# A transformer kernel on one core: the exponentials' buffers split into two rings, and the planner that orders the work given new margins

## The chip, the core and the metric

The kernel runs on one NeuronCore of a Trainium2 chip. TensorE (PE) multiplies matrices into PSUM (eight banks of 128 x 512 fp32), VectorE (DVE) and ScalarE (ACT) read PSUM and write on-chip memory (SBUF), GpSimd (POOL) works on SBUF alone, and SyncE (SP) issues most DMA transfers. The metric is the device time of one execution in microseconds (us); lower is better. The time given for a kernel is the median of several runs.

## The reference, cut to what matters

Two layers, each attention and then a gated feed-forward, with the same weights twice. x is 2048 x 512, there are 32 heads of 16, and F is 1792.

```python
for _ in range(2):
    h = layernorm(x)
    q, k, v = split_heads(h @ wqkv)                    # 32 heads of 16
    p = softmax(q @ k.T * 16 ** -0.5)                  # 2048 x 2048 per head
    x = x + merge_heads(p @ v) @ wo
    h = layernorm(x)
    x = x + (gelu_tanh(h @ w_gate) * (h @ w_up)) @ w_down
```

The exponentials are the bulk of it: 32 heads x 2048 x 2048 in each layer, 268 million in all.

## The kernel before, in words

**Tiles and units.** A *tile* is the scores of 128 keys against 512 queries of one head, one PSUM bank. A *unit* is a block of 512 queries and a group of four heads: 16 key tiles x 4 heads = 64 tiles. A layer has 4 x 8 = 32 units, the kernel 64 units and 4096 tiles. The last eight units are run as two halves of 256 queries each (parts F0 and F1), where a tile holds two key tiles of 256 queries. The four heads of a group lie in four strips of 32 rows of the PE array (j = 0 to 3), so up to four score matmuls (L1548) run side by side.

**Score slots and the two ways to an exponential.** Banks 0-2 and 3-4 are two *slots*, filled in turn with three and two tiles. ACT takes a whole slot in one instruction (L1562), 128 x 1536 or 128 x 1024, and writes bf16 exponentials to `fPT`. A fill can carry one tile more, in a bank of its own (5 or 6), which is VectorE's: L1602 turns the scores into int16 that, read as float16, are a piecewise linear exponential (`fPI`), and L1642 makes three shifted copies of up to four such tiles at once (`fPP`). Which tiles may go this way is fixed (`d_able`: every third, 20 of 64), and whether one does is decided by `vector_tile`. A tile of ACT needs one PV matmul (L1694, exponentials times V, with a 17th column of ones for the softmax's sums), a tile of VectorE needs four (one from `fPI`, three from `fPP`). PV matmuls of the four heads run side by side in four column strips and accumulate in bank 7.

**Partial sums.** When a unit's last PV matmul is done, DVE copies bank 7 to a buffer of `fOS` (L1000; L995 adds a part that was stored before). From there DMAs store it (`oscr`), gather its sums (`fLT`), and DVE inverts these; `fRB` is the inverse spread back over the rows, and POOL multiplies (L956). The buffer is free again when its four stores have landed. In layer 2 the first twelve units are begun before the last block of layer 1 is done: their part A goes to DRAM (`ascr`) and comes back into an `fOS` buffer for part B.

**Feed-forward pieces.** After the attention of a block of 512 queries, a *post* works off its output projection, layer norm, gate (L1222, evacuated by L1241), gelu (L1509 on ACT, after all 14 gate tiles), up (L1222, evacuated by L1265), and down (L1286, with one bank held over seven pieces of two matmuls: an *open down tile*). A post is cut into *pieces* of mostly four 512-column matmuls, which PE runs between the fills of the next block's attention. After the last exponential comes the feed-forward of the last half block (F1), with gelu in ScalarE's evacuation (L1244).

**The planner.** The order of the instructions on each engine is not written out. `_emit_fast` runs a loop (from L1844) that keeps a modelled clock for each engine, picks what PE does next, and emits it; DVE, POOL and SP get their jobs in modelled order of readiness. What is emitted is a fixed program: each engine runs its list in order and waits on semaphores for true dependencies. So the constants of the model change the order of the program and nothing else. The ones that the change touches:
- `dma` and `turn` (L282 to L297): the modelled landing of a transfer, which decides when work that needs it is put into the order.
- `vector_tile` (L1400): a DVE tile is taken while DVE's modelled backlog, with 0.39 us for every waiting shift, is under `DVE_LATE`. `pick` (L1422) also asks that `behind() < LAG`.
- `behind` (L1808): by how much (in us of PE work) the running post is behind its even pace (`PACE`, `LAST`).
- the loop's choices (L1865 to L1912): a fill goes as soon as its slot and its `fPT` buffer are free; else PE may work until `limit`, which is the later of the next fill's readiness and ScalarE's modelled end less 0.6 us. PV rounds come first if they fit (`fit`) and if four full rounds are there; then a piece, if it fits within `limit` plus a tolerance (`p.tol`, `post_tol`); then the PV that is left; then, if the array's density over the last 3.4 us is under `DENSE`, `keep_clock` (L1708): four matmuls of zeros (L1714, *fillers*), which keep TensorE's clock up.
- `fPT` has seven buffers of 1536, and each slot takes the next one, whether it has two tiles or three; `fOS` has seven.

Of the kernel before, what the change touches and what calls it, by code (L numbers as in the profile page):

```python
# [6 lines left out]
BF = mybir.dt.bfloat16  # L7
# [168 lines left out]
def _emit_fast(nc, es, x_in, wqkv, wo, wg, wu, wd, out, n_rep=2):  # L176
# [24 lines left out]
    DVE_LATE = 2.0  # L201
# [29 lines left out]
    NPT = 7  # L231
    PT = sb("fPT", [128, NPT, 1536], BF)
# [6 lines left out]
    NOS = 7  # L239
# [39 lines left out]

    wire = [0.0]  # L280

    def dma(eng, grp, dst, src, r=(), w=(), serial=False, kb=32):  # L282
        if grp not in sch.groups:
            sch.add_dma_group(grp, serial=serial)
        t = max(sch.free[eng], sch.ready(eng, r, w)) + 0.5
        wire[0] = max(t, wire[0]) + kb / 280.0
        return sch.op(eng, lambda e: e.dma_start(dst, src), r=r, w=w, grp=grp, cost=0.5, lat=wire[0] - t + 1.3)
# [3 lines left out]
    def turn(grp, dst, src, r, w):  # L291
        if grp not in sch.groups:
            sch.add_dma_group(grp, serial=True)
        t = max(sch.free["sp"], sch.ready("sp", r, w)) + 1.2
        wire[0] = max(t, wire[0]) + 128 / 180.0
        return sch.op("sp", lambda e: e.dma_start_transpose(dst, src), r=r, w=w, grp=grp, cost=1.2,
                      lat=wire[0] - t + 0.6)  # L297
# [286 lines left out]
    def xn(i, alt):  # L584
        if alt == "late":
            return PT[:, i, 0:D].bitcast(F16)
        return HT[:, i + 4 * alt, 0:D].bitcast(F16)
# [791 lines left out]
    LAG = 16.8  # L1379
    PRE = 1  # L1380
    pt_no = [0]
    dg = {"n": 0, "items": [], "uk": None, "done": [0]}
# [80 lines left out]
    def fill_ready():  # L1463
# [11 lines left out]
        if pend.get(("PT", pt_no[0] % NPT)):  # L1475
            return None
# [53 lines left out]
    def a_slot(atiles, dtile):  # L1530
# [6 lines left out]
        p = pt_no[0] % NPT  # L1537
# [24 lines left out]
        o = sch.op("act", lambda e: e.activation(PT[:, p, 0:512 * na].rearrange("p (a b) -> p a b", a=na),  # L1562
# [15 lines left out]
        for k, x in enumerate(atiles):  # L1578
            add(x, o.seen, PT[:, p, 512 * k:512 * (k + 1)], [("PT", p)], ("PT", p))
# [196 lines left out]
    def post_source():  # L1776
        while True:
            if posts:
# [62 lines left out]
    DENSE = 0.7  # L1841
    log = {"idle": 0.0, "warm": 0}

    while True:  # L1844
# [25 lines left out]
        stuck[0] = F is None and not (pend.get(("PT", pt_no[0] % NPT)) and left())  # L1870
# [12 lines left out]
        press = F is None and left() and pend.get(("PT", pt_no[0] % NPT)) or shifts and pend.get(("PP", shifts[0][0]))  # L1883
# [891 lines left out]
```

## Time and profile before

| | us |
|---|---|
| median of 9 runs (1609.57 to 1613.55) | 1612.09 |
| the profiled execution, its own time | 1615.17 |
| its span, first to last instruction | 1613.3 |
| VectorE busy | 1420.0 (88%) |
| GpSimd busy | 179.1 (11%) |
| first exponential starts / last one ends | 17.88 / 1578.34 |
| matmuls of zeros (L1714) | 1420 |
| score matmuls that ACT's fills and DVE's tiles come from (L1548) | 4608 |
| PV matmuls from `fPT`, `fPP`, `fPI` | 3589, 3057, 1019 |
| mean granted TensorE clock | 0.995 |

The page gives, for each engine, busy time and share of the span; then slices of the span, the DMA queues, the chain of work that ended last, and groups of instructions by line, with the mean length of one in ns and the idle time of the engine just ahead of them. "Busy" of a group is time covered, so instructions that overlap on an engine count once, while a mean is each one's own length. A waiting time put down to "PE fPS L1548" means that the scores came late. "Issue" is time without a wait that the trace shows. 16 DMA engines move 70 GB/s on average, and their packets fill about a quarter of their time.

### The profile page before, as it was taken

The numbers are of one execution on the slowest core, as the hardware profiler recorded it, in microseconds if no ns is written. First come the engines' busy times: TensorE is split into PE (matmuls) and PEld (weight loads), VectorE is DVE, ScalarE is ACT, GpSimd is POOL, SyncE is SP. The second block draws the span as 40 slices with busy tenths as digits, with TensorE's granted clock in tenths as the row PEclk, the third lists the DMA queues.
The fourth block names the chain that finished last, engine by engine and source line by source line (L and its number), as shares of the span: only waits on it lengthen the run. The fifth ranks groups of instructions, "written<-read, shape, count | busy, mean of one in ns | idle before, by whom it ended". The sixth has DMA issues, their size and how long they took to land.

```text
span 1613.3 us, 38435 instructions
## 1 busy us (share of the span) xinstructions
PE 1521.3 (94%) x16176; PEld 505.9 (31%) x16176; DVE 1420.0 (88%) x2428; ACT 1535.4 (95%) x1321; POOL 179.1 (11%) x218
## 2 busy tenths in 40 slices
PE   8999999998999999999999999889999999999998
PEld 3332222222222222332332223222222222444445
DVE  7899999879989899888999889998888988998784
ACT  6999999999999999999999999999999999999992
POOL 3311010011100021001411001010001000200000
PEclk8999999999999999999999999999999999999999
DMA  5200111233111251123311233332313113213235
GB/s 154 60 5 8 49 35 48 56 87 78 47 47 38 65 122 34 38 60 104 87 47 60 66 97 75 88 102 76 99 35 96 48 50 114 61 44 88 64 98 156
DMA packets 168376, 112.39 MB, mean 70 GB/s; under 512 B 55048, under 2 KB 148232, under 8 KB 168200
## 3 DMA queue, kind: packets, MB, share of 16 engines
q1 hardware_dynamic: 164504, 105.28, 24.5%
q0 software_dynamic: 2112, 4.19, 1.0%
q8 instruction: 131, 2.15, 0.6%
q10 hardware_dynamic: 1584, 0.39, 0.1%
q14 instruction: 45, 0.37, 0.1%
HBM read 81.40 MB, written 19.78 MB: 63 GB/s over the span
## 4 chain that ended last, share of the span: by engine, by line
ACT 43%; PE 42%; DVE 10%; DMA 2%; issue 1%; POOL 1%; SPq 0%; DVEq 0%; POOLq 0%
ACT fPT L1562 39%; PE fPS L1694 13%; PE fPS L1548 12%; PE fPS L1222 8%; PE fPS L1286 5%; DVE fPI L1602 4%; DVE fPP L1642 4%; PE fPS L653 3%; ACT fHT L1509 3%; DMA fRB<-rscr 1%; PE fPS L1714 1%; DMA fXNT<-fHT 1%; ACT L1509 1%; ACT L1562 0%; PE fPS L730 0%
## 5 line engine op out<-in xcount | busy, mean ns | idle before, releaser
L1562 ACT ACTIVATE fPT<-fPS 128x1536 bf16<-128x1536 f32 x1276 | 1459.0, 1281 | 39.9 <-PE fPS L1548 34.9
L1602 DVE TENSOR_SCALAR fPI<-fPS 128x512 int16<-128x512 f32 x908 | 616.6, 685 | 88.8 <-PE fPS L1548 82.5
L1548 PE MATMUL fPS<-fQ,fKT 32*128 32x512 f16 (+1 forms) x4608 | 510.9, 360 | 52.7 <-ACT fPT L1562 34.2
L1642 DVE TENSOR_SCALAR fPP<-fPI 128x2048 int16<-128x2048 int16 (+3 forms) x753 | 471.7, 654 | 9.4 <-PE fPS L1694 4.4
L1694 PE MATMUL fPS<-fPT,fVP 128*17 128x512 bf16 (+1 forms) x3589 | 465.0, 359 | 10.8 <-DVE fOS L995 3.7
L1694 PE MATMUL fPS<-fPP,fVD 128*17 128x512 f16 (+1 forms) x3057 | 424.6, 358 | 3.9 <-DVE fPP L1642 2.6
L1548 PEld LDWEIGHTS fPS<-fQ,fKT 32*128 32x128 f16 x4608 | 137.2, 91 | 531.4 <-ACT fPT L1562 376.4
L1694 PE MATMUL fPS<-fPI,fVP 128*17 128x512 f16 (+1 forms) x1019 | 266.1, 359 | 1.6 <-DVE fOS L1000 0.9
L1222 PE MATMUL fPS<-fXNT,fWR 128*128 128x512 f16 (+1 forms) x952 | 220.3, 363 | 8.2 <-DVE fHT L1265 3.5
L1694 PEld LDWEIGHTS fPS<-fPT,fVP 128*17 128x17 f16 x3589 | 120.1, 88 | 146.7 <-issue 92.3
L1694 PEld LDWEIGHTS fPS<-fPP,fVD 128*17 128x17 f16 x3057 | 116.2, 89 | 117.4 <-issue 59.3
L956 POOL TENSOR_TENSOR fAT<-fOP,fRB 128x512 f16<-128x512 f32 (+1 forms) x35 | 41.9, 1197 | 850.8 <-DMA fRB<-rscr 839.8
L1286 PE MATMUL fPS<-fWR,fHT 128*128 128x512 bf16 x428 | 118.7, 383 | 0.3 <-DVE fPI L1602 0.2
L1714 PE MATMUL fPS<-fONB,fZV 128*17 128x512 f16 x1420 | 117.2, 386 | 1.5 <-POOL fQMASK L380 1.5
L1222 PEld LDWEIGHTS fPS<-fXNT,fWR 128*128 128x128 bf16 x952 | 77.0, 98 | 112.4 <-DVE fPI L1602 26.3
L1265 DVE TENSOR_TENSOR fHT<-fPS,fHT 128x512 bf16<-128x512 f32 x112 | 76.4, 689 | 37.0 <-PE fPS L1222 26.9
L1241 DVE CAST fHT<-fPS 128x512 bf16<-128x512 f32 x105 | 71.5, 686 | 16.8 <-PE fPS L1222 16.8
L1694 PEld LDWEIGHTS fPS<-fPI,fVP 128*17 128x17 f16 x1019 | 67.4, 89 | 38.0 <-issue 18.5
L743 POOL TENSOR_SCALAR fVD<-fVP 128x544 f16<-128x544 f16 (+1 forms) x48 | 57.1, 1190 | 167.6 <-DVE fVP L751 165.0
L605 POOL TENSOR_SCALAR fLNS<-fMV 128x2 f32<-128x2 f32 (+1 forms) x28 | 11.6, 416 | 363.8 <-DVE fMV L596 363.3
L1000 DVE COPY fOS<-fPS 128x512 f32<-128x512 f32 (+1 forms) x72 | 45.1, 626 | 7.6 <-PE fPS L1694 6.5
L701 DVE TENSOR_SCALAR fQ<-fPS,fQMASK 128x512 f16<-128x512 f32 (+1 forms) x72 | 46.3, 684 | 1.3 <-PE fPS L653 1.2
(89 smaller groups left out, 638.8 us busy)
## 6 DMA issues: line engine op xcount, KB each, us to landing
fWR<-in_B_w_up_dram SPq DMA_DIRECT2D x62, 256.0 KB, 2.9
fWR<-in_B_w_down_dram SPq DMA_DIRECT2D x58, 256.0 KB, 2.8
fWR<-in_B_w_gate_dram SPq DMA_DIRECT2D x57, 256.0 KB, 4.9
oscr<-fOS SPq DMA_DIRECT2D x224, 32.0 KB, 1.7
fOP<-oscr SPq DMA_DIRECT2D x28, 256.0 KB, 2.8
fRB<-rscr SPq DMA_DIRECT2D x28, 256.0 KB
fX<-in_A_x_dram POOLq DMA_DIRECT2D x4, 1024.0 KB, 6.4
xscr<-fX SPq DMA_DIRECT2D x16, 256.0 KB, 2.1
```

The lines of the kernel that those rows point to most:

```text
L743: job("pool", 2, [(lambda e, dst=dst, src=src, ph=ph: e.tensor_scalar(dst, src, 2.0 ** (-ph / NPH), None, op0=ALU.mult), [("VP", c, k) for ...
L1222: ins = e.matmul(bank(bs[0])[:, w * qn:(w + 1) * qn], lhsT=wchunk(s, (ft + w) % 2, ck), rhs=XNT[:, ck, xs], start=(ck == 0), stop=(ck == N ...
L1241: evac_job(1, b, [(lambda e: e.tensor_copy(in_ht(ft), in_bank(b)), [BK[b]], fk, 0.6)], got(("gate", layer, qb, h, ft)))
L1265: (lambda e: e.tensor_tensor(in_ht(ft), in_bank(b), in_ht(ft), op=ALU.mult), [BK[b]] + fk, fk, 0.62)], got(("up", layer, qb, h, ft))))
L1286: ins = e.matmul(bank(b)[:, 0:D], lhsT=HT[:, ft, i * 128:(i + 1) * 128], rhs=wslot(s)[:, jj * D:(jj + 1) * D], start=(ft == 0), stop=(ft = ...
L1509: sch.op("act", lambda e, lo=lo, hi=hi: e.activation(HT[:, lo:hi, q0:q0 + qn], HT[:, lo:hi, q0:q0 + qn], ACTF.Gelu_apprx_tanh), r=keys, w= ...
L1548: ins = e.matmul(bank(b)[:, b0:b0 + qn], lhsT=KT[32 * j:32 * j + 32, (x[1] % NG) // 2, kt * 128:(kt + 1) * 128], rhs=Q[32 * j:32 * j + 32, ...
L1562: o = sch.op("act", lambda e: e.activation(PT[:, p, 0:512 * na].rearrange("p (a b) -> p a b", a=na), PS[:, b0:b0 + na, :], ACTF.Exp, scale ...
L1602: dve(0, [(lambda e: e.tensor_scalar(PI[:, gi, 512 * r:512 * (r + 1)], bank(bd), DBIAS, 0.0, op0=ALU.add, op1=ALU.max), [BK[bd]], [("PI", ...
L1642: shifts.append((s, [(lambda e: e.tensor_scalar(PP[:, s, 0:512 * n], PI[:, gi, 0:512 * n], int(OCT) * ph // NPH, None, op0=ALU.add), [("PI ...
L1694: ins = e.matmul(PS[32 * j:32 * j + VW, ACC, 0:qn], lhsT=l, rhs=r_, start=a, stop=z, tile_position=(0, 32 * j), skip_group_check=True)
L1714: ins = e.matmul(PS[32 * j:32 * j + VW, ACC, :], lhsT=ZV[:, :], rhs=ones, start=False, stop=False, tile_position=(0, 32 * j), skip_group_c ...
```

## The change

It makes these edits:
- `fPT`: five buffers of three tiles and five of two, in two rings, instead of seven of three. Odd and even slots take from their own ring: ten slots are held instead of seven, in 25 tiles of SBUF instead of 21.
- `fOS`: four buffers instead of seven.
- The model's transfers land 0.8 us later, its transposing ones 1.5 us later (`SAFE`, `SAFE_T`).
- `DVE_LATE` 2.0 to 2.83, the price of a waiting shift 0.39 to 0.37, `LAG` 16.8 to 24: when VectorE gets a tile.
- A group of DVE tiles is closed when fewer than three of its segment's tiles are left, not four.
- `limit` runs to 0.44 us ahead of ScalarE's end instead of 0.6, and `fit` no longer rounds up; at most four PV rounds go at once, not six.
- `post_tol` is 1.58 us for a post that is behind and 0.01 for one that isn't (0.42 and 0.27 before); the first nine pieces of a post have the tolerance of 1.0, not eight; `PACE` and `LAST` move.
- A piece that holds a bank and is ready, and that fits, goes ahead of PV.
- `DENSE` 0.70 to 0.67.

```diff
-    DVE_LATE = 2.0
+    DVE_LATE = 2.83
...
-    NPT = 7
-    PT = sb("fPT", [128, NPT, 1536], BF)
+    NPT3, NPT2 = 5, 5
+    PT = sb("fPT", [128, 3 * NPT3 + 2 * NPT2, 512], BF)
...
-    NOS = 7
+    NOS = 4
...
+    SAFE, SAFE_T = 0.8, 1.5
...
-        return sch.op(eng, lambda e: e.dma_start(dst, src), r=r, w=w, grp=grp, cost=0.5, lat=wire[0] - t + 1.3)
+        return sch.op(eng, lambda e: e.dma_start(dst, src), r=r, w=w, grp=grp, cost=0.5, lat=wire[0] - t + 1.3 + SAFE)
...
-                      lat=wire[0] - t + 0.6)
+                      lat=wire[0] - t + 0.6 + SAFE_T)
...
-    LAG = 16.8
+    LAG = 24
...
+    def pt_of():
+
+        n = pt_no[0] // 2
+        return NPT3 + n % NPT2 if pt_no[0] % 2 else n % NPT3
...
-        late += 0.39 * len(shifts)
+        late += 0.37 * len(shifts)
...
-        p = pt_no[0] % NPT
+        p = pt_of()
+        at = 3 * min(p, NPT3) + 2 * max(0, p - NPT3)
...
-        if dg["items"] and (len(dg["items"]) == 4 or seg_left[dg["uk"]] < 4 and not any(
+        if dg["items"] and (len(dg["items"]) == 4 or seg_left[dg["uk"]] < 3 and not any(
...
-                        if first <= 8:
+                        if first <= 9:
...
-    LAST = 2 * NU - NG / 2 + 1.5
+    LAST = 2 * NU - NG / 2 + 2.31
...
-    PACE = [(NU + 1.0, A_END - 1.03)]
+    PACE = [(NU + 1.0, A_END - 1.2)]
...
-        return 0.42 if behind() > 0 else 0.27
+        return 1.58 if behind() > 0 else 0.01
...
-    DENSE = 0.7
+    DENSE = 0.67
...
-            limit = max(F, sch.free["act"] - 0.600) - t
+            limit = max(F, sch.free["act"] - 0.44) - t
...
-        fit = int((limit - change("col")) / MM + 0.3)
+        fit = int((limit - change("col")) / MM + 0.00)
...
-        if fit >= 1 and (full >= want or full and (rest or press)):
-            pv(its, min(fit, full, 6))
+        keep = next((p for p in (src.peek() for src in sources) if p is not None and p.held is not None), None)
+        ready_ = keep is not None and piece_ready(keep, keep.held) <= t + 0.02 and keep.cost + change("full") <= limit + 0.1
+        if not (ready_ and not press) and fit >= 1 and (full >= want or full and (rest or press)):
+            pv(its, min(fit, full, 4))
             continue
```

The program that comes out holds these counts, instruction lists of both kernels set side by side:

| | before | after |
|---|---|---|
| ACT exponentials of 1536, 1024, 512 | 637, 638, 1 | 631, 632, 0 |
| ACT table loads of this path | 18 | 16 |
| DVE tiles (L1602) | 908 | 939 |
| DVE shifts (L1642) of 2048, 1536, 1024, 512 | 585, 66, 84, 18 | 627, 51, 57, 42 |
| PV matmuls of 512 columns from `fPT`, `fPP`, `fPI` | 2787, 2391, 797 | 2766, 2454, 818 |
| PV matmuls of 256 columns from `fPT`, `fPP`, `fPI` | 802, 666, 222 | 782, 726, 242 |
| matmuls of zeros (L1714) | 1420 | 1044 |
| score, projection, feed-forward matmuls; transfers by kind | | as before |

Two of the places where the orders differ matter below. In the program before, the gelu of half block F0 stands on ACT's list ahead of the last exponentials (five slots follow it), and three of F0's seven up pieces follow the last scores on PE's list. In the changed program that gelu stands after the last exponential, and after the last scores PE has three gate and all seven up pieces of F0 still to do, and 32 matmuls of zeros in two groups.

More of the change, by code (lines that the diff above doesn't have):

```diff
@@ L585, in xn @@
         if alt == "late":
-            return PT[:, i, 0:D].bitcast(F16)
+            return PT[:, 3 * i, 0:D].bitcast(F16)
         return HT[:, i + 4 * alt, 0:D].bitcast(F16)
@@ L1474, in fill_ready @@
             return None
-        if pend.get(("PT", pt_no[0] % NPT)):
+        if pend.get(("PT", pt_of())):
             return None
@@ L1561, in a_slot @@
         bks = [BK[b] for b in banks[:na]]
-        o = sch.op("act", lambda e: e.activation(PT[:, p, 0:512 * na].rearrange("p (a b) -> p a b", a=na),
+        o = sch.op("act", lambda e: e.activation(PT[:, at:at + na, :],
                                                  PS[:, b0:b0 + na, :], ACTF.Exp, scale=1.0 / (OCT * LOG2E)),
@@ L1578, in a_slot @@
         for k, x in enumerate(atiles):
-            add(x, o.seen, PT[:, p, 512 * k:512 * (k + 1)], [("PT", p)], ("PT", p))
+            add(x, o.seen, PT[:, at + k, :], [("PT", p)], ("PT", p))
         if dtile is not None:
@@ L1869, in _emit_fast @@
         limit = 99.0
-        stuck[0] = F is None and not (pend.get(("PT", pt_no[0] % NPT)) and left())
+        stuck[0] = F is None and not (pend.get(("PT", pt_of())) and left())
         if F is not None:
-            limit = max(F, sch.free["act"] - 0.600) - t
+            limit = max(F, sch.free["act"] - 0.44) - t
         its = pv_ready(t)
         byj = [sum(1 for it in its if it[1] == j) for j in range(4)]
-        fit = int((limit - change("col")) / MM + 0.3)
+        fit = int((limit - change("col")) / MM + 0.00)
         full = min(byj)
@@ L1882, in _emit_fast @@
                 full = max(byj)
-        press = F is None and left() and pend.get(("PT", pt_no[0] % NPT)) or shifts and pend.get(("PP", shifts[0][0]))
+        press = F is None and left() and pend.get(("PT", pt_of())) or shifts and pend.get(("PP", shifts[0][0]))
         if press and its:
```

## The prediction, as it was put on record

> **What bounds the kernel now.** I read the page's busy times first, then the ScalarE groups kept apart by shape, then the waits, then the busy times of a window cut at the first and last exponential, and last ScalarE's timeline, for the pace inside a stall-free run and for the end.
>
> Busy times of the page:
>
> ```profile
> PE 1521.3 (94%) x16176; PEld 505.9 (31%) x16176; DVE 1420.0 (88%) x2428; ACT 1535.4 (95%) x1321; POOL 179.1 (11%) x218
> ```
>
> PE and ACT look alike here, but PE's share holds 1420 matmuls of zeros that need not be there, and a busy PE is not a full one. ACT's share is real. The groups by shape (busy us, mean ns of one, idle ahead of it):
>
> ```profile
> L1562 ACT ACTIVATE fPT<-fPS 128x1536 bf16<-128x1536 f32 x637 | 950.8, 1493 | 30.4 <-PE fPS L1548 26.7
> L1562 ACT ACTIVATE fPT<-fPS 128x1024 bf16<-128x1024 f32 x638 | 682.5, 1070 | 9.6 <-PE fPS L1548 8.1
> L1602 DVE TENSOR_SCALAR fPI<-fPS 128x512 int16<-128x512 f32 x908 | 616.6, 685 | 88.8 <-PE fPS L1548 82.5
> ...
> L1642 DVE TENSOR_SCALAR fPP<-fPI 128x2048 int16<-128x2048 int16 x585 | 396.3, 704 | 4.8 <-PE fPS L1694 0.8
> ```
>
> ACT waits for nothing but late scores. Between 17.9 and 1578.4 us, from the first exponential to the last, the window gives length and then PE, PEld, DVE, ACT, POOL:
>
> ```profile
> 17.90:1578.40 1560.50, 1477.78 (x15832) 479.81 (x15832) 1391.52 (x2362) 1526.69 (x1309) 170.20 (x191) 1.00 0.25 65
> ```
>
> So ACT is idle for 1560.5 - 1526.7 = 33.8 us of that window and DVE for 169.0. The program is a head of 17.9 us, a middle as long as ScalarE's work plus 33.8 us, and a tail of 34.9 us after the last exponential, which is PE's. ScalarE's timeline, stall-free stretch and end (start, length):
>
> ```profile
> 487.46 57.02 ACT L1562 ACTIVATE fPT<-fPS 128x1536 bf16<-128x1536 f32 x50
> ...
> 1566.70 1.28 ACT L1509 ACT_TABLE_LOAD   x1
> 1567.99 3.28 ACT L1509 ACTIVATE fHT<-fHT 128x1792 bf16<-128x1792 bf16 x2
> 1571.29 1.28 ACT L1562 ACT_TABLE_LOAD   x1
> 1572.59 5.75 ACT L1562 ACTIVATE fPT<-fPS 128x1024 bf16<-128x1024 f32 x5
> 1578.35 1.28 ACT L1860 ACT_TABLE_LOAD   x1
> ```
>
> 50 instructions, 25 of each size, in 57.02 us: 2.281 us a pair, although the means add to 2.563, since they overlap by 0.14 us each. A pair saved is worth 2.281 us.
>
> **ScalarE's part, on the path.** The program after the change has 6 instructions of 1536, 6 of 1024 and the one of 512 fewer: 31 tiles, which VectorE's 908 to 939 take up. Worth 6 x 2.281 = 13.7 us, and for the 512 its 0.898 us less an overlap of 0.14: 0.76. Together 14.4 us. F0's gelu, now behind the last exponential, takes 3.28 us out of the middle, and with it two table loads of 1.28 us vanish: 5.8 us. The middle becomes 1560.5 - 14.4 - 5.8 = 1540.2 us if ScalarE's idle time stays 33.8.
>
> **The tail, on the path.** Before, PE did 24 matmuls of F0's up after the last scores, now 24 of gate and 56 of up: 56 more, seven pieces at 0.97 us (the chain has pieces of eight at 0.97 to 0.99) = 6.8 us. PV after the last fill is 48 matmuls of 256 instead of 40: two rounds of 0.108, 0.2 us. The 32 zeros in the tail are 8 rounds, of 0.22 us each in the timeline: 1.8 us, and they stand where PE waits for evacuations. The gelu needs the last gate evacuated by DVE (0.69) and the evacuation of up needs the gelu: 0.7 + 3.3 us, beside which PE has PV, two up pieces, the closing of the last unit and the output projection, some 7 us by the same pieces of the tail before. I count 0.4 us of it as seen. Sum: +9.2 us (from 6.8, all waits hidden, to 13, the gelu seen in full). Tail 34.9 + 9.2 = 44.1.
>
> **VectorE, beside it.** By busy us for one of each row (0.679 for a tile; 0.677, 0.545, 0.418, 0.272 for shifts of 2048 to 512): 31 x 0.679 + 42 x 0.677 - 15 x 0.545 - 27 x 0.418 + 24 x 0.272 = +36.6 us. In the middle DVE goes from 1391.5 of 1560.5 us (89.2%) to 1428.1 of 1540 (92.7%), its idle time from 169 to 112. I price it at nothing, because that idle time covers it on average. If the cover is gone, scores and pieces wait behind a late evacuation, since PE runs its list in order and banks 5 and 6 come back only from DVE.
>
> **PE, beside it.** 123 more PV matmuls, 63 of 512 and 60 of 256: 16 rounds of 0.216 and 15 of 0.108 us, +5 us. 376 fewer zeros: 94 rounds, -20 us. Score matmuls and pieces are the same. Both lie in PE's free time.
>
> **Margins and order.** I cut PE's list at the score fills and priced what stands between two by its rows (PV round 0.216 us, change of kind 0.107, piece 0.97). Gaps of over 1.1 us, more than an average exponential leaves, number 132 before and 138 after; without the long gaps beside the gelus their excess adds up to about 33 us in both. So the new tolerances (none for a post in time, more for a late one), the earlier `limit`, and the cap of four rounds move planned lateness about, and I give them nothing; from -5 to +8 us, as the excess could fall on short or long exponentials. The nine-piece tolerance, the moved paces and the held down piece have the same answer: they order the same pieces.
>
> **Rings.** No ACT instruction waits for PV in the waits: all its 34.9 us there are for late scores. A full ring would show as exactly that, because the planner holds the fill back; what speaks against a full ring is that PE fills up to the limit with zeros, which are emitted only when no full PV round is ready and fits. Deeper rings are worth 0 to -10 us; I take 0. `fOS` with four: a buffer is held for copy (0.69), gather, four stores and landing (1.7 us), some 6 us, and a unit lasts about 25; only in layer 2's part B, at 1015 to 1080 us, units close every 5.5 us, where a buffer is also held for the 3.0 us of its load. That makes two or three in use: nothing, at most a late load of 3 us for each of 12 units that PV's ring then covers.
>
> **Transfers.** Placed later, work meets fewer late landings. The waits show little to gain: 2.5 us for PE's gate behind transposing DMAs, 1.9 behind POOL's multiply. 0 to -4 us; I take 0. In the head, 32 more zeros stand ahead of the first projections; PE waited there for data or an evacuation anyway, and more activity may lift the clock (0.71 in the head) sooner: -1.5 to +1, taken as 0.
>
> [...] The row first: the clock was 0.995 over the span, and even with 1420 zeros two windows of 10 us, at 1040 and 1050, had 0.93 and 0.89, a loss of (0.07 + 0.11) x 10 = 1.8 us. [...] 94 rounds less over 1560 us are 1.3% of the array's time, so I take the row.
>
> **The sum.** 17.9 + 1540.2 + 44.1 = 1602.2 us of span instead of 1613.3: -11.1. The profiled execution took 1615.2, 1.9 more than its span and 3.1 more than the median of the runs. The same difference on the median: 1612.1 - 11.1 = 1601.0 us.
>
> **The rivals.**
> - *The stalls shrink too* (0.20). Deeper rings, later transfers and tighter tolerance take a third to two thirds of the 33.8 us. For it: the largest stalls, 2.7, 1.6, 1.3 us, are single events of late evacuations. Against: DVE is fuller, and the planner's gaps hold the same excess. At -14 us: 1587.
> - *VectorE becomes the bound* (0.10), the slower end. For it: at 1000 to 1100 us DVE was busy for 93.6 us already and ACT's idle time was 3.9 us of that stretch, against 2.1 us per 100 in the middle as a whole; a backlog of 2.83 instead of 2.0 us lets each of 939 tiles hold its bank for up to 0.8 us longer. If one in 30 of the 939 makes PE, and then ACT, wait that long, it costs 25 us: 1601 + 25 = 1626; it decides against the change from 11 us, one in 70. Against it: at 700 to 800 us ACT was idle for 4.2 us with DVE at 87%, so DVE's load alone doesn't set the stalls.
> - *The gain is given back* (0.08). The tail is at its 13 us and the stalls grow by 7: 1612, no change.
> - *The rings do nothing* and all comes from moved thresholds: same time, so it lies in the forecast. The tile counts cannot tell it apart; a run of the new thresholds with the old rings would.
>
> **How the numbers follow.** Forecast 0.62: 1601, alone 1594 to 1608. Faster: 0.62 + 0.20 = 0.82; same 0.08; slower 0.10. About 0.2% is what a measurement can tell from no change here. The range takes the forecast, most of the shrinking stalls down to 1587, and half of the gain given back: up to 1611.
>
> **What would show it.** Right: ACT's middle about 20 us shorter with its idle time near 34; last exponential near 1558; a tail of 44 with the gelu in it; DVE near 93% of the middle. Wrong: ACT idle in the middle under 25 or over 45 us; waits of PE's loads behind L1602 and L1642 (26.3 us ahead of L1222 and 40.1 ahead of L1694 before) half as long again; a head that differs by over 1 us; a clock below 0.99.

## The result

The changed kernel takes 1599.1 us (median of 10 runs, 1597.26 to 1601.01), the kernel before on the same chips 1612.4 (31 runs, 1608.48 to 1616.3). The ratio is 0.9919, 95% interval 0.9911 to 0.9927: faster by 13 us, where 11.1 were forecast. In three experiments further down (late transfers alone, the loop's margins undone, the held down tile behind PV) a second, general program ran behind the first, as the kernel has it for softmax sums or variances outside set limits. Of those only the first program is read, in one execution. Why the limits were passed there, with the same inputs, stays open, so these three are weak witnesses.

The profiled execution of the changed kernel took 1605.6 us, 6.5 more than the median of its runs, for a reason that its clock shows below. Its page gives busy time, share and instructions of each engine:

```profile
PE 1512.4 (94%) x15923; PEld 499.6 (31%) x15923; DVE 1438.2 (90%) x2483; ACT 1520.8 (95%) x1306; POOL 179.0 (11%) x218
```

The groups kept apart by shape (busy us, mean ns of one, then idle time ahead):

```profile
L1569 ACT ACTIVATE fPT<-fPS 128x1536 bf16<-128x1536 f32 x631 | 936.2, 1484 | 31.1 <-PE fPS L1555 27.4
L1569 ACT ACTIVATE fPT<-fPS 128x1024 bf16<-128x1024 f32 x632 | 669.0, 1059 | 7.8 <-PE fPS L1555 6.6
L1609 DVE TENSOR_SCALAR fPI<-fPS 128x512 int16<-128x512 f32 x939 | 635.8, 684 | 61.6 <-PE fPS L1555 57.7
...
L1649 DVE TENSOR_SCALAR fPP<-fPI 128x2048 int16<-128x2048 int16 x627 | 425.6, 701 | 7.9 <-PE fPS L1701 5.0
```

And the window from the first exponential to the last (length, then PE, PEld, DVE, ACT, POOL, clock):

```profile
14.80:1559.10 1544.30, 1461.68 (x15439) 468.07 (x15439) 1404.78 (x2412) 1508.74 (x1291) 168.30 (x189) 0.99 0.25 65
```

ACT's work in the middle fell from 1526.7 to 1508.7 us; its idle time is 1544.3 - 1508.7 = 35.6, and was 33.8. The head ends at 14.8 us instead of 17.9, and the tail is 1603.8 - 1559.1 = 44.7 us instead of 35.0. So the span of the profile went -3.1 in the head, -18.0 in ACT's work, +1.8 in its idle time and +9.7 in the tail, -9.5 together.

Idle time that looks unchanged hides one thing. Windows of the clock show it (the column after POOL is the granted clock):

```profile
1010.00:1020.00 10.00, 9.20 (x72) 1.72 (x72) 7.88 (x13) 8.02 (x8) 0.00 (x0) 0.57 0.25 56
1020.00:1030.00 10.00, 9.48 (x72) 1.73 (x68) 7.05 (x12) 7.11 (x7) 0.00 (x0) 0.57 0.36 94
1030.00:1040.00 10.00, 8.76 (x101) 2.30 (x97) 9.85 (x18) 10.00 (x10) 0.00 (x0) 1.00 0.32 81
1040.00:1050.00 10.00, 8.88 (x58) 1.74 (x56) 7.13 (x13) 7.08 (x7) 1.27 (x1) 0.66 0.50 125
```

PE reads "busy" for 9.2 of 10 us at a clock of 0.57, with 72 matmuls done; ACT is idle for 2.0 + 2.9 + 2.9 = 7.8 us in the three cold windows. The timed runs had clocks of 0.998 to 1.000, this execution 0.992. The same program less 32 matmuls of zeros in its head (the seventh experiment, below called the *twin*) has clock 1.00 there. Its first of these windows and its middle:

```profile
1010.00:1020.00 10.00, 7.98 (x92) 1.97 (x86) 9.92 (x17) 10.00 (x10) 0.00 (x0) 1.00 0.33 80
```

```profile
16.80:1552.80 1536.00, 1442.88 (x15386) 467.85 (x15439) 1403.92 (x2411) 1507.62 (x1291) 170.39 (x189) 1.00 0.25 65
```

So in the twin PE does 92 matmuls in 7.98 us, ACT is idle for 28.4 us in the middle, and the tail is the same 44.7. For the timed runs it is the better witness of the middle: there the idle time shrank by about 5 us. Part of that may be the execution of before, which was itself some 3 us slower than its median.

### The profile page after: what moved, and what is told of

Same layout as the page of the kernel before. It is cut to its first block, busy times and chain, and to the rows that moved or that the text cites. A ratio compares the mean times of both kernels' runs of the same rounds, so it can differ in the third digit from the quotient of the medians.

```text
span 1603.8 us, 38014 instructions
## 1 busy us (share of the span) xinstructions
PE 1512.4 (94%) x15923; PEld 499.6 (31%) x15923; DVE 1438.2 (90%) x2483; ACT 1520.8 (95%) x1306; POOL 179.0 (11%) x218
## 4 chain that ended last, share of the span: by engine, by line
ACT 39%; PE 36%; DVE 23%; issue 1%; DMA 0%; SPq 0%; DVEq 0%
ACT fPT L1569 36%; PE fPS L1701 11%; PE fPS L1555 10%; DVE fPI L1609 10%; DVE fPP L1649 8%; PE fPS L1223 7%; PE fPS L1287 4%; PE fPS L654 2%; ACT fHT L1515 2%; DVE fHT L1242 1%; PE fPS L1721 1%; DVE fOS L1001 1%; DVE fHT L1266 1%; DVE fQ L702 1%; PE fPS L731 1%
## 5 line engine op out<-in xcount | busy, mean ns | idle before, releaser
L1609 DVE TENSOR_SCALAR fPI<-fPS 128x512 int16<-128x512 f32 x939 | 635.8, 684 | 61.6 <-PE fPS L1555 57.7
L1649 DVE TENSOR_SCALAR fPP<-fPI 128x2048 int16<-128x2048 int16 (+3 forms) x777 | 488.7, 653 | 12.2 <-PE fPS L1701 8.9
L1701 PE MATMUL fPS<-fPT,fVP 128*17 128x512 bf16 (+1 forms) x3548 | 459.3, 361 | 6.1 <-DVE fOS L1001 2.5
L1701 PE MATMUL fPS<-fPP,fVD 128*17 128x512 f16 (+1 forms) x3180 | 432.7, 359 | 5.1 <-DVE fPP L1649 3.5
L1701 PE MATMUL fPS<-fPI,fVP 128*17 128x512 f16 (+1 forms) x1060 | 273.0, 359 | 1.9 <-DVE fOS L1001 0.6
L1223 PEld LDWEIGHTS fPS<-fXNT,fWR 128*128 128x128 bf16 x952 | 77.1, 98 | 116.2 <-DVE fPI L1609 31.3
L1266 DVE TENSOR_TENSOR fHT<-fPS,fHT 128x512 bf16<-128x512 f32 x112 | 76.4, 688 | 31.2 <-PE fPS L1223 21.8
L1721 PE MATMUL fPS<-fONB,fZV 128*17 128x512 f16 x1044 | 85.0, 392 | 1.5 <-POOL fQMASK L381 1.5
L606 POOL TENSOR_SCALAR fLNS<-fMV 128x2 f32<-128x2 f32 (+1 forms) x28 | 7.9, 284 | 408.9 <-DVE fMV L597 408.6
L1515 ACT ACTIVATE fHT<-fHT 128x3584 bf16<-128x3584 bf16 (+1 forms) x16 | 47.3, 2995 | 1.2 <-DVE fHT L1242 1.1
```

Source lines behind the costliest of these rows:

```text
L1223: ins = e.matmul(bank(bs[0])[:, w * qn:(w + 1) * qn], lhsT=wchunk(s, (ft + w) % 2, ck), rhs=XNT[:, ck, xs], start=(ck == 0), stop=(ck == N ...
L1266: (lambda e: e.tensor_tensor(in_ht(ft), in_bank(b), in_ht(ft), op=ALU.mult), [BK[b]] + fk, fk, 0.62)], got(("up", layer, qb, h, ft))))
L1515: sch.op("act", lambda e, lo=lo, hi=hi: e.activation(HT[:, lo:hi, q0:q0 + qn], HT[:, lo:hi, q0:q0 + qn], ACTF.Gelu_apprx_tanh), r=keys, w= ...
L1609: dve(0, [(lambda e: e.tensor_scalar(PI[:, gi, 512 * r:512 * (r + 1)], bank(bd), DBIAS, 0.0, op0=ALU.add, op1=ALU.max), [BK[bd]], [("PI", ...
L1649: shifts.append((s, [(lambda e: e.tensor_scalar(PP[:, s, 0:512 * n], PI[:, gi, 0:512 * n], int(OCT) * ph // NPH, None, op0=ALU.add), [("PI ...
L1701: ins = e.matmul(PS[32 * j:32 * j + VW, ACC, 0:qn], lhsT=l, rhs=r_, start=a, stop=z, tile_position=(0, 32 * j), skip_group_check=True)
```

## The experiments

All compared with the kernel before on the same chip. "First" is the start of the first exponential; work and idle are ACT's between the first and last exponential of the profiled execution, tail what follows; clock is the mean over that execution, and "profiled" its own time. Where that lies some us off the median, the columns behind it do too.

| kernel | median us, ratio (95%) | profiled | first | work | idle | tail | clock |
|---|---|---|---|---|---|---|---|
| before | 1612.4 | 1615.2 | 17.9 | 1526.7 | 33.8 | 35.0 | 0.995 |
| after | 1599.1, 0.9919 (0.9911 to 0.9927) | 1605.6 | 14.8 | 1508.7 | 35.6 | 44.7 | 0.992 |
| thresholds alone | 1628.2, 1.0092 (1.0071 to 1.0113) | 1627.2 | 16.7 | 1512.3 | 46.5 | 50.0 | 0.995 |
| rings alone | 1615.2, 1.0019 (1.0010 to 1.0028) | 1611.6 | 16.9 | 1531.5 | 25.4 | 36.1 | 0.998 |
| rings and thresholds | 1613.4, 1.0006 (0.9996 to 1.0016) | 1612.7 | 16.8 | 1509.8 | 34.6 | 49.7 | 0.997 |
| after, one ring of seven | 1618.1, 1.0034 (1.0024 to 1.0044) | 1616.2 | 14.7 | 1509.3 | 48.0 | 42.6 | 0.998 |
| after, rings of four and four | 1618.4, 1.0032 (1.0021 to 1.0043) | 1616.4 | 14.7 | 1509.8 | 47.7 | 42.4 | 0.999 |
| after, 32 zeros fewer in the head | 1600.3, 0.9924 (0.9911 to 0.9937) | 1599.9 | 16.8 | 1507.6 | 28.4 | 44.7 | 0.998 |
| after, no zeros behind the head | 1619.1, 1.0043 (1.0027 to 1.0059) | 1613.5 | 14.6 | 1509.8 | 43.8 | 43.0 | 0.982 |
| after, VectorE padded | 1600.8, 0.9929 (0.9916 to 0.9943) | 1599.5 | 14.6 | 1508.5 | 30.7 | 44.0 | 1.000 |
| after, transfers as before | 1610.8, 0.9987 (0.9979 to 0.9994) | 1612.4 | 15.5 | 1513.1 | 33.4 | 48.5 | 0.993 |

One limit holds for all that change a constant of the planner: it plans everything anew from there, so such a run shows an edit's worth in this setting, and the worths don't add. The three that only drop or add instructions of a finished list are free of this.

**The new thresholds alone, in the kernel before.**

```diff
-    DVE_LATE = 2.0
+    DVE_LATE = 2.83
-        late += 0.39 * len(shifts)
+        late += 0.37 * len(shifts)
-    LAG = 16.8
+    LAG = 24
-  seg_left[dg["uk"]] < 4
+  seg_left[dg["uk"]] < 3
```

> The kernel before with VectorE's four thresholds of the change alone (backlog 2.83, shift 0.37, LAG 24, groups closed at 3). Its lists hold 934 DVE tiles (26 more than before), ACT's 631 of 1536, 634 of 1024 and one of 512, and two table loads fewer. If ScalarE's work sets the time (my theory): 6 x 1.354 + 4 x 0.928 = 11.8 us of exponentials and 5.8 us of gelu and loads leave the middle, the tail grows by some 9: about 8.6 us faster than before, 1604. If rings and late transfers made the gain by shrinking stalls: no more than 3 us faster, 1609 or above. If VectorE becomes the bound without the other margins: slower than before.

Measured: 1628.2, slower than before. 934 tiles went to DVE and ACT's work fell by 14.4 us, as it should; but its idle time grew by 12.7 and the tail by 15. My theory, that all comes from the thresholds and rings add nothing, falls. Two single stalls hold most of the added idle time, 4.98 us at 116.85 and 4.38 at 832.09; only the second is one of a full ring, as the counts further down show.

**The two rings alone** (five and five, `fOS` of four, in the kernel before).

> The kernel before with the two rings of fPT and four fOS buffers alone. Its lists hold 893 DVE tiles, 15 fewer, and 640 and 641 of ScalarE's two sizes. By my theory 3 x 1.354 + 3 x 0.928 = 6.8 us slower, 1619, if depth is worth nothing. If depth shrinks stalls by a third or more of 33.8 us: 1608 or below.

Measured: 1615.2, between the two expectations. In the profiled execution the idle time falls to 25.4, and of single stalls of 1 us or more in the middle two are left, where before had seven. But the planner gave DVE 893 tiles instead of 908, so ACT's work grew by 4.8, and the time with it. The 8.4 us of idle time are too many, since this execution was 3.6 us faster than its median and the one of before slower: with 4.8 more work, 1.1 more tail and 1.0 less head, the medians (2.4 us apart) leave some 2 to 3 us for it. The ring is worth something; alone it is given back.

**Late transfers alone** (0.8 and 1.5 us added to the modelled landings, in the kernel before).

> The kernel before with transfers modelled 0.8 and 1.5 us later alone. Its lists hold 893 DVE tiles and 1524 zeros. By my theory plus 6.8 us for ScalarE's 15 tiles, minus some 3 us if the head gets more zeros and so a warm clock: about 1616. If late modelling removes stalls by itself: 1608 or below, with ScalarE's idle time in the middle under 25 us.

Its first program has ACT's work at 1531.3 (893 tiles again), idle 31.2 and, from the last exponential to the last residual add, 31.8 us against 31.9. Its whole time says nothing, since the second program ran (4440.8). By the first, the head is 3.7 us shorter (14.2), idle falls by 2.6 and work grows by 4.6: 1.7 us ahead of before at the last add, no more than executions of before differ by.

**The changed kernel with one ring of seven.**

```diff
-    NPT3, NPT2 = 5, 5
-    PT = sb("fPT", [128, 3 * NPT3 + 2 * NPT2, 512], BF)
+    NPT = 7
+    PT = sb("fPT", [128, 3 * NPT, 512], BF)
```

> The changed kernel with one ring of seven three-tile buffers as before, the rest as changed (four fOS buffers too). Its lists hold 941 DVE tiles, 631 and 631 of ScalarE's sizes. By my theory the same as the changed kernel within 3 us, 1597 to 1602. If the deeper rings carry the gain: 1606 or above.

Measured: 1618.1; 19 us of the change are gone. The window of its middle, beside that of after (1508.74 of 1544.30) above:

```profile
14.70:1571.90 1557.20, 1458.61 (x15544) 474.63 (x15606) 1412.88 (x2419) 1509.23 (x1290) 169.46 (x191) 1.00 0.25 65
```

The same work for ACT, at a clock of 1.00, and 48.0 us of idle time: 19.6 more than the twin's 28.4. ACT's timeline of this kernel shows where (start, length, and in brackets the idle time ahead):

```profile
569.31 6.88 ACT L1568 ACTIVATE fPT<-fPS 128x1024 bf16<-128x1024 f32 x6 [3.11 <-PE fPS L1554]
...
959.95 5.54 ACT L1568 ACTIVATE fPT<-fPS 128x1024 bf16<-128x1024 f32 x5 [2.00 <-PE fPS L1554]
...
1230.99 10.49 ACT L1568 ACTIVATE fPT<-fPS 128x1536 bf16<-128x1536 f32 x9 [2.04 <-PE fPS L1554]
...
1415.76 4.82 ACT L1568 ACTIVATE fPT<-fPS 128x1536 bf16<-128x1536 f32 x4 [2.70 <-PE fPS L1554]
```

Nine stalls of 1 us or more behind the first exponential, 17.2 us together; in the twin of after there are two, 2.6 us. Each line only says "the scores came late". What held them back stands on PE's timeline, here ahead of the stall that ends at 569.31:

```profile
564.77 1.24 PE L1720 MATMUL fPS<-fONB,fZV 128*17 128x512 f16 x13
566.53 0.39 PE L1700 MATMUL fPS<-fPP,fVD 128*17 128x512 f16 x2 [0.53 <-DVE fPP L1648]
567.90 0.38 PE L1700 MATMUL fPS<-fPT,fVP 128*17 128x512 bf16 x1 [0.98 <-DVE fOS L1001]
...
568.55 0.40 PE L1700 MATMUL fPS<-fPT,fVP 128*17 128x512 bf16 x4
568.87 0.61 PE L1554 MATMUL fPS<-fQ,fKT 32*128 32x512 f16 x7
```

and on DVE's for the same stretch:

```profile
565.46 1.62 DVE L1648 TENSOR_SCALAR fPP<-fPI 128x1024 int16<-128x1024 int16 x2
567.06 0.69 DVE L1001 COPY fOS<-fPS 128x512 f32<-128x512 f32 x1
567.67 1.28 DVE L1648 TENSOR_SCALAR fPP<-fPI 128x2048 int16<-128x2048 int16 x2
```

A unit ends. Its last PV waits for two shifts that a full DVE makes late (until 566.5); then bank 7 must be copied by DVE (until 567.7); only then can the next unit's PV start and read the exponentials that fill the ring, and only behind four rounds of it do the scores of seven tiles at once (L1554 x7) reach PE. Ahead of the late shifts PE fills the time with zeros. Seven of the nine stalls, 14.0 us, end in this way: DVE's copy of bank 7, a run of PV from `fPT`, and at once a score fill. But only two of them (569.31 and 1415.76) have zeros ahead and PE waiting for the copy. In the other five, 8.2 us, PE is still in a piece when the copy ends, and comes to PV 0.4 to 0.8 us later. So it is ahead of the stall that ends at 959.95, where the copy ended at 957.9:

```profile
956.71 1.90 PE L1287 MATMUL fPS<-fWR,fHT 128*128 128x512 bf16 x8
...
959.51 0.61 PE L1554 MATMUL fPS<-fQ,fKT 32*128 32x512 f16 x6
```

Seven tiles at a blow, both slots waiting, are a mark of a full ring, but a fill behind a full ring can also have three tiles or six. That the ring was full at all seven, the planner's own count shows, below the run of four and four.

**Rings and thresholds together**, in the kernel before: all but the loop's margins, `PACE`, `LAST` and `DENSE`, the order of the held down tile and the late transfers.

> The kernel before with both rings, four fOS buffers and VectorE's four thresholds, nothing else of the change. Its lists hold 934 DVE tiles and ScalarE's 631, 634 and one. New theory: the thresholds take ScalarE's work off, and the depth of the rings is the cover that they need at a unit's end, so together ScalarE's idle time in the middle is 25 to 35 us (46.5 with the thresholds alone), and with the tail longer by some 10 us the time is about 1602 to 1606. If the two merely add up from the runs alone (+15.4 and +2.4 us): about 1630. If the tolerances, late transfers and the held down tile are what makes it work: 1612 or above.

Measured: 1613.4, no difference from before. Against the thresholds alone the idle time is back from 46.5 to 34.6, as expected; against after, 14 us are missing, so the time is that of the last expectation. Set beside the twin: ACT's work +2.2, idle +6.2 (three single stalls of 4.8, 3.5 and 2.6 us, at 117, 809 and 1551 us, hold more than that), tail +5.0. The first of them stood already with the thresholds alone, and no ring cures it (first line, thresholds alone):

```profile
116.85 34.11 ACT L1562 ACTIVATE fPT<-fPS 128x1024 bf16<-128x1024 f32 x30 [4.98 <-PE fPS L1548]
```

```profile
117.01 34.11 ACT L1568 ACTIVATE fPT<-fPS 128x1024 bf16<-128x1024 f32 x30 [4.80 <-PE fPS L1554]
```

In both, PE's list has PV, the end of a unit and eight projection matmuls, four of them for queries, ahead of the scores.

**Rings of four and four.**

```diff
-    NPT3, NPT2 = 5, 5
+    NPT3, NPT2 = 4, 4
```

> The changed kernel with two rings of four (eight slots) instead of five (ten). Its lists hold 941 DVE tiles and 631 and 631 of ScalarE's. New theory: depth pays by degrees at a unit's end, so the time lies between the changed kernel and the one with seven slots (1618): 1605 to 1613, idle time in the middle 37 to 45 us. If splitting the ring is what counts and not its depth: 1597 to 1602.

Measured: 1618.4, idle 47.7: eight slots are no better than seven, where I expected a part of the way. The idle time is cut up differently (eight stalls of 1 us or more, 11.3 us).

How much of this is a full ring can be counted. The planner's loop knows when a fill's slot and banks are free and only its `fPT` buffer is not; the fill is then held back. The n-th fill of the plan is the n-th exponential on ACT's timeline, so ACT's idle time just ahead of the held fills can be read from the trace:

| kernel | slots | fills held | held in the model, us | ACT idle ahead of them, us |
|---|---|---|---|---|
| before | 7 | 12 | 9.7 | 5.2 |
| thresholds alone | 7 | 18 | 20.5 | 13.9 |
| after, one ring of seven | 7 | 16 | 25.1 | 16.7 |
| after, four and four | 8 | 10 | 13.1 | 9.9 |
| rings alone | 10 | 0 | 0 | 0 |
| rings and thresholds | 10 | 2 | 5.5 | 4.4 |
| after | 10 | 1 | 1.0 | 0.8 |

At the held fills depth does pay by degrees: 16.7, 9.9 and 0.8 us with seven, eight and ten slots. That is most of the 19.6 us that seven slots cost against the twin, and half of the 19.3 of eight; the rest lies at fills that no ring held, and comes with the new plan. All seven stalls named above are of held fills.

**The head without its new zeros.** The finished program of after, less the 32 matmuls of zeros that it has more than before ahead of the first exponential.

```diff
+            if o.zero is not None and not o.sig and o.zero in (11, 12, 15, 16, 17, 18, 19, 20):
+                continue
             ins = o.fn(eng)
```

> The changed kernel's program, less the 32 matmuls of zeros that it has more than the kernel before ahead of the first projections; nothing else moves. If those zeros bring the first exponential forward by keeping the clock up: granted clock in the head near 0.7, first exponential near 17.9 us instead of 14.8, and 3 us more time (1602). If the earlier start had another cause, such as the loads: first exponential within 0.5 us of 14.8 and no change.

Measured: the first exponential is back at 16.81. It is the first expectation by its cause, with a smaller amount. The window from 12 to 16 us, in before, in after and in this kernel:

```profile
12.00:16.00 4.00, 3.98 (x14) 1.77 (x15) 3.30 (x8) 0.00 (x0) 1.26 (x2) 0.50 1.11 343
```

```profile
12.00:16.00 4.00, 3.92 (x33) 1.93 (x32) 3.93 (x10) 1.18 (x1) 1.26 (x2) 1.00 1.12 341
```

```profile
12.00:16.00 4.00, 4.00 (x20) 2.20 (x19) 2.56 (x6) 0.00 (x0) 1.26 (x2) 0.50 1.11 340
```

PE is "busy" for the whole of it each time, with 14, 33 and 20 matmuls at clocks of 0.50, 1.00 and 0.50. Four projection matmuls take 1.87 us in before and 1.02 in after:

```profile
12.02 1.87 PE L653 MATMUL fPS<-fXNT,fWK 128*128 128x512 f16 x4 [0.79 <-ACT fXNT L635]
```

```profile
11.58 1.02 PE L654 MATMUL fPS<-fXNT,fWK 128*128 128x512 f16 x4
```

The zeros ahead of the projections buy 2.0 us of the head's 3.1; the other 1.1 are not explained by this run. On the medians it is 1.2 us, which the intervals don't tell from nothing.

**No zeros behind the head.** The same, with `o.zero > 20`: 84 of the 1044 matmuls of zeros are left.

> The changed kernel's program without the matmuls of zeros after the head (all but 21 rounds, where no other engine waits on them); no other instruction moves. If the zeros are what holds the clock in stretches where PE is thin: the granted clock in the middle falls below 0.98, ScalarE's idle time grows, and the time rises by 5 us or more. By my prediction's row (PE has room): within 3 us of the changed kernel.

Measured: 1619.1, 20 us slower than after; its four runs go from 1613.5 us at a clock of 0.982 (the profiled one) to 1621.0 at 0.973. Three windows of 100 us:

```profile
200.00:300.00 100.00, 89.67 (x749) 25.09 (x749) 86.27 (x150) 94.79 (x79) 6.68 (x11) 0.91 0.16 41
...
500.00:600.00 100.00, 91.67 (x867) 25.74 (x871) 92.10 (x162) 99.89 (x90) 11.55 (x14) 1.00 0.34 81
...
1400.00:1500.00 100.00, 93.45 (x1398) 39.64 (x1394) 87.56 (x155) 91.59 (x76) 6.92 (x9) 0.91 0.23 59
```

Where the clock falls to 0.91, ACT is idle for 5 and 8 us of 100; in the six such windows between 300 and 1400 us at 1.00, for 0.1 to 2.5. In all ACT waits 43.8 us, 15.4 more than the twin, and the clock lost (0.998 - 0.982) x 1611 = 26 us of full speed.

**VectorE padded.** The finished program of after, with a memset of one column ahead of every second DVE tile.

```diff
+                if k % 2 == 0:
+                    e.memset(PADT[:, k:k + 1], 0.0)
                 return e.tensor_scalar(PI[:, gi, 512 * r:512 * (r + 1)], bank(bd), DBIAS, 0.0, ...
```

> The changed kernel's program with a memset of one column on VectorE ahead of every second of its 939 tile instructions (470 of them, written to a spare tile that nobody reads); nothing else moves. It adds some 30 to 50 us to VectorE's work, about what the change itself added. If VectorE's idle time covers it, as my prediction had it: within 3 us of the changed kernel (1599). If VectorE is close to the bound, so that the change used up the cover: 10 us or more above it, ScalarE's idle time in the middle over 45 us.

The row of what was added:

```profile
L1616 DVE MEMSET fPADT<- 128x1 f16 x470 | 27.7, 59 | 0.6 <-PE fPS L1557 0.6
```

Measured: 1600.8, 1.7 us more than after, which the intervals don't tell from nothing. But the dose came out small: 27.7 us were issued, and DVE's busy time in the middle grew by 4 us only, since most of each memset lies beside its neighbours (the one of 0.06 us at 500.94 within the tile's 0.69 us from 500.92). That DVE takes up a few us more without a loss that can be measured is shown; that it would take up 30 is not.

**The loop's margins undone in after** (tolerances 0.42 and 0.27, eight pieces, `limit` 0.6 us ahead, `fit` rounded up, six rounds).

> The changed kernel with the planner's loop margins as before: tolerances 0.42 and 0.27, eight tolerant pieces, limit at 0.6 us with fit rounding up, six PV rounds; rings, thresholds, late transfers, held down tile as changed. Its lists hold 946 DVE tiles, 629 and 630 of ScalarE's and three of one tile, and all 14 gate and up pieces of F0 behind the last scores. If the margins do nothing but move lateness about, as I predicted: middle as in the changed kernel, and only the tail longer, by 4 pieces more (3.9 us) and zeros: about 1603. If they keep the middle's stalls down: ScalarE's idle time in the middle over 40 us and 1610 or above.

`PACE`, `LAST` and `DENSE` stay as changed. The second program ran (4443.1). The first has 946 tiles on DVE, ACT's work 1505.0, idle 48.3 (15.7 us of it one stall that ends at 804.9, ahead of which PE waits 2.4 us for POOL's multiply, and 6.5 us another at 72.1), and 47.8 us from the last exponential to the last residual add, against 41.4 in after. The idle time is that of the second expectation, but two stalls hold 22.2 us of it, and neither is at a full ring.

**The transfers modelled as before, in after** (`SAFE, SAFE_T = 0.0, 0.0`).

> The changed kernel with the model's transfers landing as before (both additions at zero). Its lists hold 932 DVE tiles, 632, 633 and two of ScalarE's, and 12 of F0's 14 gate and up pieces behind the last scores. By the prediction late transfers are worth 0 to 4 us: with 7 tiles more for ScalarE (about 3.5 us), some 2 us of colder head and two more pieces in the tail it comes to 1604 to 1609. If modelling transfers late is what the change lives on: 1612 or above, with single stalls of ScalarE of 3 us and more in the middle.

Measured: 1610.8, 11.7 slower than after and between the two expectations; no stall behind the first exponential is longer than 1.25 us. Only 932 tiles went to DVE and ACT's work is 1513.1, 4.4 more; the tail is 3.8 longer, the head 0.7; the idle time (33.4) lies between those of after and its twin.

**The held down tile behind PV, in after.**

```diff
-        if not (ready_ and not press) and fit >= 1 and (full >= want or full and (rest or press)):
+        if fit >= 1 and (full >= want or full and (rest or press)):
```

> The changed kernel without the rule that a ready piece that holds a bank goes ahead of PV. Its lists hold 931 DVE tiles, 633 and 633 of ScalarE's, and 13 of F0's 14 gate and up pieces behind the last scores. If the rule only orders the same pieces, as I predicted: about 4 us of exponentials and 3 us of tail more, 1603 to 1608, and ScalarE's idle time in the middle as in the changed kernel (28 to 36 us). If the rule frees a bank early and so keeps VectorE's tiles and pieces moving: idle time over 40 us and 1612 or above.

The second program ran (4439.5). The first: 931 tiles, ACT's work 1512.7, idle 38.4 (one stall of 4.7 at 810.4, ahead of a held fill), 47.5 us to the last add: between the two expectations. No version here beat the changed kernel.

## Why the prediction was right

The number was right because its large terms were, and because what I had put at nothing nearly cancelled; that it cancelled was luck. ACT's idle time in the middle, step by step and each from one profiled execution: 33.8 us before, 46.5 with the thresholds alone, 34.6 with the rings added, 28.4 with margins, paces, order and late transfers added (in the twin). Read as a sum, VectorE's deeper backlog costs some 13 us, the rings give back 12 and the rest 6, although each step is a new plan. Ahead of fills that a full ring held, the same four have 5.2, 13.9, 4.4 and 0.8 us. "Idle stays 33.8" held roughly as a sum and in none of its parts.

- **ScalarE's work**, -20.2 forecast, -18.0 measured, more than the whole net gain. ACT's timeline shows the end without the gelu in it (compare the forecast of "near 1558"):

```profile
1558.08 1.02 ACT L1569 ACTIVATE fPT<-fPS 128x1024 bf16<-128x1024 f32 x1 [0.48 <-PE fPS L1555]
1559.12 1.28 ACT L1867 ACT_TABLE_LOAD   x1
1560.41 0.20 ACT L1867 ACTIVATE fACTD<-fCM 128x1 f32<-128x1 f32 x1
1560.53 1.68 ACT L1515 ACTIVATE fHT<-fHT 128x1792 bf16<-128x1792 bf16 x1
1563.32 1.70 ACT L1515 ACTIVATE fHT<-fHT 128x1792 bf16<-128x1792 bf16 x1 [1.12 <-DVE fHT L1242]
```

  The 2.2 us short is the price of a pair: 2.281 holds only inside a run, and an exponential behind a wait loses the overlap of 0.14. ACT's waits rose from 55 to 77 in the middle, 22 x 0.14 = 3.1 us. That is the right size. After and its twin have the same list, and the twin, with 67 waits, has 1.1 us less work (10 x 0.14 = 1.4).
- **The tail**, +9.2 forecast, +9.7 measured. PE's timeline after the last scores (which end at 1558.0):

```profile
1557.97 2.79 PE L1223 MATMUL fPS<-fXNT,fWR 128*128 128x256 f16 x24
...
1562.15 0.62 PE L1701 MATMUL fPS<-fPP,fVD 128*17 128x256 f16 x16 [0.40 <-DVE fPP L1649]
1562.70 1.92 PE L1223 MATMUL fPS<-fXNT,fWR 128*128 128x256 f16 x16
...
1564.82 1.03 PE L1223 MATMUL fPS<-fXNT,fWR 128*128 128x256 f16 x8
...
1568.53 3.66 PE L1223 MATMUL fPS<-fXNT,fWR 128*128 128x256 f16 x32
1572.11 1.47 PE L1721 MATMUL fPS<-fONB,fZV 128*17 128x512 f16 x24
```

  The 56 up matmuls take 1.92 + 1.03 + 3.66 = 6.6 us (6.8 forecast), the zeros 1.47 and 0.61 (1.8 forecast). The gelu, 1560.5 to 1565.0, is hidden: the one wait seen, 0.40, is for a shift.
- **The head** was taken as 0 and gave -3.1. The mechanism was in the text ("more activity may lift the clock (0.71 in the head) sooner") with a bound of -1.5; the seventh experiment shows it at 2.0. I set the bound too close: at clock 0.50 every four projection matmuls took 1.87 us instead of 1.02. A head that differs by over 1 us was one of my signs of being wrong, and it came; of the others, the waits behind L1602 and L1642 (L1609 and L1649 after) rose from 26.3 and 40.1 to 31.3 and 50.9, less than half as long again.
- **"Deeper rings are worth 0 to -10 us; I take 0"** is the step that failed. With the old ring, or eight slots, the changed kernel is 1618, slower than before. The argument was that PE runs zeros up to the limit and so the ring isn't full. It is wrong: zeros show that no PV was ready, and at a unit's end none is, first while its last PV waits for DVE's shifts and then until bank 7 is copied, while the ring fills behind it; and in five of the seven stalls there were no zeros at all. By the held fills, 0 was off by 5.2 us with the old thresholds; the new ones made it 13.9. The same mark (seven tiles of scores behind a run of PV) stood already in the trace of before, ahead of its largest stall (2.71), which I had read as a late evacuation and no more (PE, then ACT):

```profile
794.30 0.60 PE L1694 MATMUL fPS<-fPP,fVD 128*17 128x512 f16 x7
794.83 0.65 PE L1548 MATMUL fPS<-fQ,fKT 32*128 32x512 f16 x7
```

```profile
795.27 5.54 ACT L1562 ACTIVATE fPT<-fPS 128x1024 bf16<-128x1024 f32 x5 [2.71 <-PE fPS L1548]
```

- **"The rings do nothing"**, the rival with the same time, falls with it, by the run that I had named: the thresholds alone give 1628.
- **"VectorE becomes the bound"**, the slower rival, came near what is at work there: thresholds alone, and the changed kernel with seven slots, allow DVE a deeper backlog and have 12.7 and 14.2 us more idle time than before. But it looked to a tile that holds its bank, where the runs show late shifts and the copy at a unit's end, and PE's piece beside them, behind a full ring. It does not reach the changed kernel because ten slots carry ACT over that end. That is the cover of VectorE's deeper backlog; I had named only DVE's average idle time.
- **VectorE's own work** was forecast at +36.6 us and 92.7%; its busy time over the span grew by 18.2 and is 91.0% of the middle. The counts and durations were right: the busy times of DVE's groups add to 1523.2 us before and 1558.7 after, some 35 more. The term that failed is that they add at all: what groups cover together rose from 103 us (1523.2 - 1420.0) to 120.5 (1558.7 - 1438.2).
- **Margins, paces, held down tile and transfers, "nothing" each.** Rings and thresholds without them give 1613.4, so together (with `DENSE`) they are worth 14 us here, the other half of the mistake. (The prediction calls the new `limit` earlier; it lies 0.16 us later, 0.44 instead of 0.6 ahead of ScalarE's end.) Single ones undone: the transfers cost 11.7 us; in the first programs of the other two the tail to the last add is 6 us longer, and single stalls of 5 to 16 us appear. I had compared the planner's gaps on average; by these runs what they change is where one long gap lands. How the 14 us divide among them can't be told, because each edit re-plans the rest; the paces, `DENSE` and the four `fOS` buffers have no run of their own.
- **The clock: "I take the row"** was a mistaken choice, although the zeros of the changed kernel happened to be enough: I had counted nothing for clock lost to fewer zeros. With 960 zeros gone the profiled execution took 1613.5 us at a clock of 0.982, 13.6 more than the twin's, and ScalarE waited for 15.4 of the 26 us of clock lost. The profiled execution of after lost (0.43 + 0.43 + 0.34) x 10 = 12.0 us of clock in its three cold windows, and ScalarE 7.8 of it. PE has free time on average, and still some 0.6 of the clock lost came through (15.4 of 26 and 7.8 of 12.0 us). Before has one stretch at a clock of 0.50 in its middle, 3.41 us from 1048.7; one more like it, which loses 3.41 x 0.5 = 1.7 us of clock, would by this cost about 1 us (an estimate from these two). After has two at 0.50, 17.07 us from 1011.5 and 6.83 from 1042.2. Just ahead of the first of them the clock was 1.00 and PE worked, with no gap over 0.95 us:

```profile
1008.10:1011.50 3.40, 2.33 (x26) 0.68 (x30) 3.40 (x7) 3.40 (x5) 0.00 (x0) 1.00 0.29 77
```

  PE read busy for 2.33 of 3.40 us there, for 2.43 of the 3.40 us ahead of the second, and for 2.04 of the 3.40 us ahead of the one in before. What brings the clock down in such a place, and from which load on, no run here measures.

That after's own program was cold at 1010 to 1050 us and that of its twin wasn't is not explained by an edit: the list is the same there. It varies between executions (the timed ones of after have 0.998 to 1.000).

## What to carry to other kernels

Size a buffer ring by the longest event that stops its consumer, and not by average rates alone: look at the places where a chain closes (here the last PV, the copy of its bank, the first PV of the next), and at how many slots are filled at once behind it. Filler work on an engine doesn't prove that a ring ahead of it has room. And edits of which none gains alone (here thresholds 1628, rings 1615, and the two together 1613) can need each other and the rest (1599), so test them together before one is thrown away.

## What the runs showed of the hardware that was not expected

- 32 matmuls of zeros ahead of the first projections raise the clock from 0.50 to 1.00 for the stretch of 12 to 16 us (the changed program with and without them) and bring the first exponential 2.0 us forward.
- 960 matmuls of zeros fewer, on a PE that is busy for 94% of the span by its records, cost 20 us of 1600: clock 0.973 to 0.982 instead of 0.998 to 1.000.
- A PE that reads busy for 9.5 of 10 us can stand at a clock of 0.57; and the clock went from 1.00 to 0.50, for 17.07 us, behind 3.40 us in which PE read busy for 2.33 and had no gap over 0.95 (after, at 1011.5).
- A one-column memset on DVE lasts 59 ns, and 470 of them added 4 us of busy time instead of 27.7.
